# HGRN2 attention with a cosine router: embeddings' norm first, loads in order of use, a PSUM bank for the places, a clamp inside the scan, and the last three steps written out

## The chip, the cores and the metric

The kernel runs on one core of a Trainium2 chip. The metric is the device time of one execution in microseconds (us), measured for the kernel before and after the change; lower is better. The profile is one execution recorded by the hardware profiler. Its engines are TensorE (PE for matmuls, PEld for its weight loads), VectorE (DVE), ScalarE (ACT), GpSimd (POOL) and SyncE (SP, which issues most transfers). A name with a q behind it (SPq, ACTq, POOLq) is an engine's instruction queue.

## The reference

```python
def _attn_ref(q, k, v, f_logit):          # (4, 8, 768, 48): batch, heads, steps in time, head size
    f = 1.0 / (1.0 + np.exp(-f_logit))
    for t in range(S):
        state = f[:, :, t, :, None] * state + np.einsum('bhd,bhe->bhde', k[:, :, t], v[:, :, t])
        y[:, :, t] = np.einsum('bhd,bhde->bhe', q[:, :, t], state)

def _moe_ref(x, expert_emb, tau, w1, w2): # x: 3072 rows of 384, 8 experts, hidden size 1024
    xn = x / (np.linalg.norm(x, axis=-1, keepdims=True) + 1e-06)
    en = expert_emb / (np.linalg.norm(expert_emb, axis=-1, keepdims=True) + 1e-06)
    logits = xn @ en.T / tau
    expert_idx = np.argmax(logits, axis=1)
    gate_w = softmax(logits)[np.arange(N), expert_idx]
    for e in range(E):
        mask = expert_idx == e
        h = np.maximum(x[mask] @ w1[e], 0.0)
        out[mask] = gate_w[mask, None] * (h @ w2[e])
```

Gated linear attention gives 3072 rows of 384 numbers; each row goes to the one expert whose embedding is nearest by cosine, and comes back weighted by its gate. All data is fp32.

## The kernel before

The work is cut into 24 steps: six chunks of 128 positions, and in each chunk the four batches; step i is chunk i // 4 of batch i % 4, with all eight heads. Within a chunk the recurrence is turned into matrix products; a state of 48 by 48 per head is carried from chunk to chunk of a batch, that is, from step i to step i + 4.

Per step, by function: `load` brings f, k, q and v (192 KB each) by four transfers on SP. `decays` transposes f on TensorE (L676), takes its sigmoid on ACT into `f_T` (L684), and a scan on VectorE from the back forms the suffix products `suf` (L686). Their first column per head pair, the decay of the whole chunk, is clamped from below at `PC_MIN` into `pc_all` (L690), and its reciprocal (L694) starts the forward scan `at` (L700, `decays2`). `keys` transposes k, copies it out on ACT (`kraw`, L722) and multiplies it by `suf` on POOL into `kz` (L724). `queries` multiplies the transposed q by `at` into `qa` (L732). `carry` multiplies the incoming state by the chunk's decay on POOL (`old`, L709) and copies it on ACT into two halves of `st` (L714). `scores` multiplies `kz` by `qa` (L742) and masks on VectorE (`am`, L745). `outputs` multiplies `st` and v with `qa` and `am` into `f_y` (L788, L794), copied to `f_xT` on ACT (L799; `xT` below). `update` and `update2` transpose `kz` again (L757), copy it (`kt`, L759), multiply it by v into PSUM tile `add` (L770) and form the new state (`new`, L778).

Routing: `rows_out` turns `f_xT` back into rows together with the logits (L805, PSUM tile `misc`) and copies them out on ACT (`f_xg`, L811; squares, L813); `logits` sums the logits on VectorE (L817). After each group of steps (four, later two and one) `route` and `count` find the experts and the running counts on VectorE (L828 to L844; one copy on ACT), `place` counts the places of the group's rows by two matmuls (L851, L852, also in `misc`) and two VectorE operations (L854, L856), and `scatter` sends one step's rows to their place in `x_sorted` by an indirect transfer on POOL (L861). PSUM has eight banks: three for `tp`, and one each for `misc`, two `sc`, `add` and `f_y`.

The order is written out by hand: `as_written` keeps every engine to the program's order, and the loop at L983 calls the functions above for steps i + 2 down to i - 2, so a step passes through four rounds. In round i POOL gets the `kz` of step i + 1, one scatter and `old` of step i; the embeddings' norm and the tables of the router are worked out in round -1 (`tables`, `embeddings`). The norm (L914 to L924) uses a square on ACT and, on VectorE, four Newton steps for the root.

After the last step the expert stage follows: for each of eight experts its 448 places are read from `x_sorted` (L1048), transposed (L1057), multiplied by w1 (L1089) and w2 (L1103), and scattered to the output (L1118). Its first transposes wait for all rows. A flag (L1027 to L1039) starts a general path if an expert has too many rows or a decay was clamped; with these inputs it is not taken.

```python
                for i in range(-2, LAST + 1):
                    at(i + NLD, lambda j: load(j) if j >= NLD - 1 else None)
                    at(i + 2, decays)
                    at(i, update)
                    at(i + 1, keys)
                    at(i - 2, rows_out)
                    at(i + 1, queries)
                    at(i + 2, decays2)
                    at(i, carry)
                    at(i, scores)
                    at(i - 1, outputs)
                    at(i, update2)
```

Of the kernel before, what the change touches and what calls it, by code (L numbers as in the profile page):

```python
# [10 lines left out]
FP32 = mybir.dt.float32  # L11
# [534 lines left out]
def kernel(  # L546
# [53 lines left out]
    with ExitStack() as fast:  # L600
# [43 lines left out]
        with tc.tile_pool(name="f_fix", bufs=1) as fix, tc.tile_pool(name="f_work", bufs=2) as work, tc.tile_pool(  # L644
# [11 lines left out]
            cnt_ps = misc[:, HP * RW + B * E : HP * RW + B * E + E]  # L656
            bad_ps = misc[:, HP * RW + B * E + E : HP * RW + B * E + E + 1]
# [8 lines left out]
            def load(i):  # L666
                b, c = steps[i]
                for nm, src in (("f", f_logit), ("k", k), ("q", q), ("v", v)):
                    dst = lds[nm][i % len(lds[nm])][:, :, 0:DH]
                    nc.sync.dma_start(out=dst, in_=src[b, :, c * P : c * P + P].rearrange("h p d -> p h d"))  # L670
                live[i]["v"] = lds["v"][i % NV]
# [7 lines left out]
            def decays(i):  # L679
# [82 lines left out]
            def update2(i):  # L762
# [4 lines left out]
                add = ps_s.tile([P, HP, DH], FP32, name="add")  # L767
# [78 lines left out]
            def place(g):  # L846

                s0, n = groups[g]
                rank = misc[:, HP * RW : HP * RW + n * E].rearrange("p (e b) -> p e b", e=E)
                before = hots[g] if n == 1 else upto[g]  # L850
                nc.tensor.matmul(rank, lhsT=tri, rhs=hots[g][:, :, 1:], start=True, stop=False)  # L851
                nc.tensor.matmul(rank, lhsT=ones, rhs=before[:, :, 0:n], start=False, stop=True)  # L852
# [22 lines left out]
            def pads(j):  # L875
                for nm in "fkqv":
                    if j < len(lds[nm]):
                        nc.vector.memset(lds[nm][j][:, :, DH:64], 30.0 if nm == "f" else 0.0)

            def blanks(t):  # L880
                nc.gpsimd.memset(t, 0.0)

            def first():
                warm = work.tile([1, 1], FP32, name="f_warm", bufs=1)
                nc.vector.memset(warm, 0.0)
                nc.scalar.activation(warm, warm, AF.Sigmoid)
                for j in range(NLD - 1):
                    load(j)
                pads(0)
                blanks(f_sb[0])  # L890
                blanks(f_sb[1])
                pads(1)
                nc.vector.memset(revone, 0.0)
                nc.vector.memset(revone[:, 0 : HP * W].rearrange("p (n w) -> p n w", w=W)[:, :, 0], 1.0)
                nc.vector.memset(revone[:, HP * W : HP * W + 1], 1.0)
                blanks(fwd1[0])
                blanks(f_sb[2])
                blanks(fwd1[1])
                make_upper_triangular(nc, causal, val=1.0, diag=True)
                for j in range(2, NV):  # L900
                    pads(j)
                nc.vector.memset(emb[:, :, DH:64], 0.0)
                nc.scalar.dma_start(out=emb[:, :, 0:DH], in_=moe_expert_emb.rearrange("e (h d) -> e h d", h=H))
                nc.scalar.dma_start(out=tau, in_=moe_tau.to_broadcast([P, 1]))

            def embeddings():

                rtau = work.tile([P, 1], FP32, name="f_rtau", bufs=1)
                esq = work.tile([E, H, 64], FP32, name="f_esq", bufs=1)
# [266 lines left out]
```

## Time and profile before

| | us |
|---|---|
| median of 3 runs | 536.28 (536.28 to 536.43) |
| the profiled execution | 536.07 |
| its span, first to last instruction | 534.2 |
| TensorE matmuls busy | 476.6 (89%) |
| VectorE busy | 209.4 (39%) |
| ACT busy | 155.9 (29%) |
| POOL busy | 111.6 (21%) |
| mean granted TensorE clock | 0.963 |

The span is counted from the first instruction; the execution takes 1.87 us more. The busy shares are means over stages of different kind: TensorE's 89% holds in the expert stage as in the steady loop, while VectorE, ACT and POOL do most of their work in the first 200 us. What bounds a stage is read from its order of time: which wait ends last there. A row of the timeline gives the start in us from the span's start, the duration (of merged neighbours: from the first start to the last end), engine, line, operation, what it writes and reads, how many were merged, and, in brackets, the idle time of the engine before it with what ended that. A matmul's end is modelled; starts are firm. "issue" as the releaser means that the profile names none.

### The profile page before, as it was taken

The numbers are of one execution on the slowest core, as the hardware profiler recorded it, in microseconds if no ns is written. First come the engines' busy times: TensorE is split into PE (matmuls) and PEld (weight loads), VectorE is DVE, ScalarE is ACT, GpSimd is POOL, SyncE is SP. The second block draws the span as 40 slices with busy tenths as digits, with TensorE's granted clock in tenths as the row PEclk, the third lists the DMA queues.
The fourth block names the chain that finished last, engine by engine and source line by source line (L and its number), as shares of the span: only waits on it lengthen the run. The fifth ranks groups of instructions, "written<-read, shape, count | busy, mean of one in ns | idle before, by whom it ended". The sixth has DMA issues, their size and how long they took to land.

```text
span 534.2 us, 7556 instructions
## 1 busy us (share of the span) xinstructions
PE 476.6 (89%) x2968; PEld 314.4 (59%) x2968; DVE 209.4 (39%) x492; ACT 155.9 (29%) x330; POOL 111.6 (21%) x131
## 2 busy tenths in 40 slices
PE   2499899999898646999999999999999999999980
PEld 2398798989897544555555555555555555555540
DVE  7799789888886224331120220220220200201000
ACT  2156455555554223221221221221221201101210
POOL 3324254545453320000020110200200200200201
PEclk9999899999998875999999999999999999999995
DMA  9999999999710115053153143233323403100101
GB/s 145 163 164 219 195 274 232 187 316 191 132 41 19 61 63 161 1 171 118 21 196 118 54 161 118 96 121 118 110 108 118 148 17 119 41 1 0 44 3 52
DMA packets 117268, 61.64 MB, mean 115 GB/s; under 512 B 101568, under 2 KB 111225, under 8 KB 117224
## 3 DMA queue, kind: packets, MB, share of 16 engines
q1 hardware_dynamic: 113424, 51.42, 42.6%
q0 software_dynamic: 3584, 9.64, 5.3%
q8 instruction: 25, 0.41, 0.4%
q14 instruction: 19, 0.16, 0.1%
q10 hardware_dynamic: 216, 0.01, 0.0%
HBM read 49.79 MB, written 12.06 MB: 116 GB/s over the span
## 4 chain that ended last, share of the span: by engine, by line
issue 33%; PE 29%; POOL 3%; ACT 1%; DMA 1%; POOLq 0%; DVE 0%; SPq 0%; ACTq 0%; DVEq 0%
PE h_ps L1089 14%; PE y_ps L1103 10%; POOL out_dram L1118 3%; PE x_tp L1057 1%; PE misc L805 1%; DMA xs<-x_sorted 1%; PE sc L742 1%; PE f_y L788 1%; PE y_tp L1115 1%; PE f_y L794 1%; DMA x_sorted<-f_xg,f_pos_i 0%; ACT f_xT L799 0%; ACT f_yo L1117 0%; ACT f_xg L811 0%; PE misc L851 0%
## 5 line engine op out<-in xcount | busy, mean ns | idle before, releaser
L1089 PE MATMUL h_ps<-xTs,w 128*128 128x448 f32 x384 | 147.6, 545 | 0.0
L1103 PE MATMUL y_ps<-hTs,w 128*128 128x448 f32 x384 | 147.2, 540 | 0.0
L1089 PEld LDWEIGHTS h_ps<-xTs,w 128*128 128x128 f32 x384 | 73.8, 192 | 72.1 <-issue 71.7
L1103 PEld LDWEIGHTS y_ps<-hTs,w 128*128 128x128 f32 x384 | 71.7, 190 | 65.4 <-issue 65.4
L1118 POOL DMA_INDIRECT out_dram<-f_yo,gtok x32 | 30.2, 942 | 296.6 <-ACT f_yo L1117 291.7
L1093 DVE TENSOR_SCALAR hTs<-h_ps 128x448 f32<-128x448 f32 x32 | 20.0, 624 | 159.3 <-PE h_ps L1089 159.3
L724 POOL TENSOR_TENSOR kz<-kraw,suf 128x512 f32<-128x512 f32 x24 | 30.5, 1272 | 92.3 <-ACT kraw L722 40.5
L1095 ACT ACTIVATE hTs<-h_ps 128x448 f32<-128x448 f32 x32 | 17.4, 543 | 104.2 <-PE h_ps L1089 104.2
L1109 ACT COPY yTs<-y_ps 128x448 f32<-128x448 f32 x16 | 8.5, 532 | 117.5 <-PE y_ps L1103 117.5
L686 DVE TENSOR_TENSOR_SCAN suf<-f_T,revone 128x517 f32<-128x517 f32 x24 | 31.6, 1317 | 16.1 <-ACT f_T L684 16.0
L805 PE MATMUL misc<-unit,f_xT 128*128 128x104 f32 x192 | 26.9, 284 | 8.0 <-ACT f_xT L799 7.7
L700 DVE TENSOR_TENSOR_SCAN at<-f_T,fwd 128x516 f32<-128x516 f32 x24 | 31.2, 1300 | 0.0
L745 DVE TENSOR_TENSOR am<-sc,causal 128x512 f32<-128x512 f32 x48 | 30.6, 677 | 1.6 <-PE sc L742 1.6
L742 PE MATMUL sc<-qa,kz 64*128 64x128 f32 x384 | 30.9, 306 | 0.0
L805 PEld LDWEIGHTS misc<-unit,f_xT 128*128 128x128 f32 x192 | 23.7, 194 | 11.3 <-ACT f_xT L799 10.8
L861 POOL DMA_INDIRECT x_sorted<-f_xg,f_pos_i x24 | 25.1, 1046 | 22.2 <-issue 13.3
L714 ACT COPY st<-old 64x192 f32<-64x192 f32 x40 | 14.0, 350 | 50.7 <-POOL old L709 44.2
L742 PEld LDWEIGHTS sc<-qa,kz 64*128 64x128 f32 x384 | 26.1, 207 | 4.4 <-issue 3.2
L794 PE MATMUL f_y<-am,f_v 128*64 128x128 f32 x384 | 25.4, 275 | 0.0
L676 PE MATMUL tp<-f_ident,f_f 128*128 128x128 f32 x96 | 17.1, 304 | 8.0 <-DMA f_f<-in_f_logit_dram 4.1
L788 PE MATMUL f_y<-qa,st 128*64 128x128 f32 x320 | 23.2, 290 | 0.0
L794 PEld LDWEIGHTS f_y<-am,f_v 128*64 128x64 f32 x384 | 21.8, 138 | 0.5
(129 smaller groups left out, 462.0 us busy)
## 6 DMA issues: line engine op xcount, KB each, us to landing
w<-in_moe_w_dram SPq DMA_DIRECT2D x16, 1536.0 KB
xs<-x_sorted SPq DMA_DIRECT2D x8, 700.0 KB
f_f<-in_f_logit_dram SPq DMA_DIRECT2D x24, 192.0 KB
f_k<-in_k_dram SPq DMA_DIRECT2D x24, 192.0 KB
f_q<-in_q_dram SPq DMA_DIRECT2D x24, 192.0 KB
f_v<-in_v_dram SPq DMA_DIRECT2D x24, 192.0 KB
x_sorted<-blank SPq DMA_DIRECT2D x1, 1600.0 KB
out_dram<-f_yo,gtok POOLq DMA_INDIRECT x32, 5.5
```

The lines of the kernel that those rows point to most:

```text
L686: nc.vector.tensor_tensor_scan(suf[:, ::-1], ft[:, ::-1], revone[:, ::-1], 0.0, ALU.mult, ALU.add)
L700: nc.vector.tensor_tensor_scan(at, L["ft"][:, 0 : HP * W], L["d1"], 0.0, ALU.mult, ALU.add)
L724: nc.gpsimd.tensor_tensor(kz, kraw, z, ALU.mult)
L742: nc.tensor.matmul(sc[par][:, hp], lhsT=kz[r, hp], rhs=qa[r, hp], start=True, stop=True)
L745: nc.vector.tensor_tensor(am[:, par], sc[par], causal.unsqueeze(1).to_broadcast([P, HP, P]), ALU.mult)
L788: nc.tensor.matmul(y[r, hp], lhsT=L["st"][:, hp, par], rhs=L["qa"][:, hp], start=hp == 0, stop=False, skip_group_check=True,)
L794: nc.tensor.matmul(y[r, hp], lhsT=L["v"][:, 2 * hp + par], rhs=L["am"][:, par, hp], start=c == 0 and hp == 0, stop=True, skip_group_check= ...
L805: nc.tensor.matmul(rows_ps[:, hp], lhsT=L["xT"][:, hp], rhs=unit[:, hp], start=True, stop=True)
L861: nc.gpsimd.indirect_dma_start(out=x_views[s][:], out_offset=bass.IndirectOffsetOnAxis(ap=pos_i[:, s : s + 1], axis=0), in_=live[s]["row"] ...
L1089: nc.tensor.matmul(ps, lhsT=w1[:, c, f * P : f * P + P], rhs=xTs[e][:, c], start=c == 0, stop=c == DC - 1)
L1103: nc.tensor.matmul(ps, lhsT=w2[:, f, d * P : d * P + P], rhs=hTs[e][:, f], start=f == 0, stop=f == FC - 1)
L1118: nc.gpsimd.indirect_dma_start(out=out_views[e * NB + j][:], out_offset=bass.IndirectOffsetOnAxis(ap=gtok[:, e, j : j + 1], axis=0), in_=y ...
```

## The change

- Start (`first`): the transfer of the embeddings goes first on SP, f of step 1 is issued from ACT's queue, tau behind it. The embeddings' norm (square, root by ACT's table and one Newton step in `inv_norm`, scaling) is done ahead of the first step on ACT and VectorE. ACT first loads the table for roots, then that for sigmoids.
- Loads: `load` brings one tensor; each round asks for k, then f of the step after, then q and v. The pads of the load buffers, the router's tables and the other constants are written in rounds -1 to 3 by `prepare`, behind the round's other work, the pads from buffer 2 on by POOL in place of VectorE. The embeddings' transposes are in round 0, in `misc`.
- Clamp: the suffix scan multiplies and takes the maximum with `revone`, whose zeros are now `PC_MIN`. The VectorE instruction at L690 is gone; the reciprocal reads `suf`, and `pc_all` is a copy on ACT, behind the sigmoid of the step.
- PSUM: `add`, the places and the counts share a bank of their own, `small`; `misc` keeps the rows and the logits. The two matmuls of `place` change places.
- Order: `carry` is called for step i + 1 and ahead of the scatter. The loop ends at round 22, and what is left of the last three steps is written out, with scatters sent as their places are known.

```diff
-            cnt_ps = misc[:, HP * RW + B * E : HP * RW + B * E + E]
+            small = ps_s.tile([P, 512], FP32, name="small")
+            add_ps = small[:, 0 : HP * DH].rearrange("p (n d) -> p n d", d=DH)
+            rank_ps = small[:, HP * DH : HP * DH + B * E]
...
                 nc.vector.tensor_tensor_scan(
-                    suf[:, ::-1], ft[:, ::-1], revone[:, ::-1], 0.0, ALU.mult, ALU.add
-                )
-                pc = pc_all[:, i]
-                nc.vector.tensor_scalar(
-                    pc, suf[:, 0 : HP * W].rearrange("p (n w) -> p n w", w=W)[:, :, 1], PC_MIN, None, ALU.max
-                )
+                    suf[:, ::-1], ft[:, ::-1], revone[:, ::-1], 0.0, ALU.mult, ALU.max
+                )
+                pc = suf[:, 0 : HP * W].rearrange("p (n w) -> p n w", w=W)[:, :, 1]
                 d1 = fwd1[i % 2]
                 nc.vector.reciprocal(d1.rearrange("p (n w) -> p n w", w=W)[:, :, 0], pc)
+                nc.scalar.copy(pc_all[:, i], pc)
...
-                rank = misc[:, HP * RW : HP * RW + n * E].rearrange("p (e b) -> p e b", e=E)
+                rank = rank_ps[:, 0 : n * E].rearrange("p (e b) -> p e b", e=E)
...
             def first():
...
+                nc.vector.memset(en, 1.0)
+                nc.scalar.activation(en[0:1, 2:3], en[0:1, 2:3], AF.Sqrt)
+                nc.sync.dma_start(out=emb[:, :, 0:DH], in_=moe_expert_emb.rearrange("e (h d) -> e h d", h=H))
+                nc.vector.memset(emb[:, :, DH:64], 0.0)
+                load("f", 0)
+                load("f", 1, nc.scalar)
+                load("k", 0)
+                load("q", 0)
+                load("v", 0)
+                load("k", 1)
+                load("f", 2)
+                load("q", 1)
+                load("v", 1)
+                for j in range(2, NLD - 1):
+                    for nm, o in (("k", 0), ("f", 1), ("q", 0), ("v", 0)):
+                        load(nm, j + o)
+                nc.scalar.dma_start(out=tau, in_=moe_tau.to_broadcast([P, 1]))
...
+                nc.vector.memset(revone, PC_MIN)
...
+                nc.scalar.activation(esq, emb, AF.Square, accum_out=en[:, 0:1])
+                nc.vector.reciprocal(rtau, tau)
+                inv_norm(en[:, 1:2], en[:, 0:1], en[:, 2:3])
+                nc.scalar.activation(esq[0:1, 0, 0:1], esq[0:1, 0, 0:1], AF.Sigmoid)
+                nc.vector.tensor_scalar(emb, emb, en[:, 1:2], rtau[0:E], ALU.mult, ALU.mult)
...
+            def prepare(i):
+
+                if i == -1:
+                    pads(2, nc.gpsimd)
+                    pads(3, nc.gpsimd)
+                if i == 0:
+                    embeddings()
+                    pads(4, nc.gpsimd)
...
             with as_written(tc):
                 first()
-                for i in range(-2, LAST + 1):
-                    at(i + NLD, lambda j: load(j) if j >= NLD - 1 else None)
+                for i in range(-2, NST - 1):
+                    if i >= -1:
+                        for nm, o in (("k", 0), ("f", 1), ("q", 0), ("v", 0)):
+                            load(nm, i + NLD + o)
...
                     at(i - 2, logits)
-                    for s in ready[: 1 if i < NST - 4 else None]:
-                        scatter(s)
-                        ready.remove(s)
-                    at(i, carry)
+                    at(i + 1, carry)
+                    send(1 if i < NST - 4 else 2)
                     at(i, scores)
                     at(i - 1, outputs)
...
                     at(i, update2)
-                for g in pend:
-                    place(g)
-                    ready += range(groups[g][0], groups[g][0] + groups[g][1])
-                for s in ready:
-                    scatter(s)
+                    prepare(i)
+                scores(NST - 1)
+                rows_out(NST - 3)
+                settle()
+                outputs(NST - 2)
+                logits(NST - 3)
+                finish(NST - 3)
+                send(2)
+                outputs(NST - 1)
+                settle()
+                rows_out(NST - 2)
+                logits(NST - 2)
+                finish(NST - 2)
+                settle()
+                send(3)
+                rows_out(NST - 1)
+                logits(NST - 1)
+                finish(NST - 1)
+                settle()
+                send(B)
```

`settle` places the groups that are counted, `send(n)` scatters up to n steps whose places are known, and `finish(i)` routes and counts a group whose last step is i.

POOL in the steady loop before, two rounds in the middle of the loop (the DMA is the scatter of one step's rows):

```order
L724 TENSOR_TENSOR kz<-kraw,suf 128x512
L861 DMA x_sorted<-f_xg_82,f_pos_i 3584x400
L709 TENSOR_TENSOR old<-new,pc_all 128x192
L724 TENSOR_TENSOR kz<-kraw,suf 128x512
L861 DMA x_sorted<-f_xg_82,f_pos_i 3584x400
L709 TENSOR_TENSOR old<-new,pc_all 128x192
```

and in the changed kernel, the same rounds:

```order
L731 TENSOR_TENSOR kz<-kraw,suf 128x512
L716 TENSOR_TENSOR old<-new,pc_all 128x192
L868 DMA x_sorted<-f_xg_81,f_pos_i 3584x400
L731 TENSOR_TENSOR kz<-kraw,suf 128x512
L716 TENSOR_TENSOR old<-new,pc_all 128x192
L868 DMA x_sorted<-f_xg_81,f_pos_i 3584x400
```

`old` has moved from behind the scatter to ahead of it.

ACT over one steady round before, from one sigmoid to the next:

```order
L684 ACTIVATE f_T_146<-tp 128x4x128
L759 COPY f_kt<-tp 128x512
L722 COPY kraw<-tp 128x512
L811 COPY f_xg_82<-misc 128x384
L813 ACTIVATE f_sq,f_xg_82<-f_xg_82 128x384
L714 COPY st_143<-old 64x4x48 x2
```

and in the changed kernel:

```order
L693 ACTIVATE f_T_148<-tp 128x4x128
L701 COPY pc_all<-suf 128x4
L766 COPY f_kt<-tp 128x512
L729 COPY kraw<-tp 128x512
L818 COPY f_xg_81<-misc 128x384
L820 ACTIVATE f_sq,f_xg_81<-f_xg_81 128x384
L721 COPY st_142<-old 64x4x48 x2
```

The copy of `pc_all` from `suf` is new and stands ahead of `kt` and `kraw`.

ACT at the start before and, in the second fence, in the changed kernel:

```order
L886 ACT_TABLE_LOAD
L886 ACTIVATE f_warm<-f_warm 1x1
L903 DMA f_emb<-in_moe_expert_emb_dram 8x8x48
L904 DMA f_tau<-in_moe_tau_dram 128x1
L684 ACTIVATE f_T_145<-tp 128x4x128
```

```order
L895 ACT_TABLE_LOAD
L895 ACTIVATE f_en<-f_en 1x1
L676 DMA f_f_128<-in_f_logit_dram 128x8x48
L910 DMA f_tau<-in_moe_tau_dram 128x1
L922 ACTIVATE f_esq,f_en<-f_emb 8x512
L628 ACTIVATE f_en<-f_en 8x1
L925 ACT_TABLE_LOAD
L925 ACTIVATE f_esq<-f_esq 1x1
L693 ACTIVATE f_T_146<-tp 128x4x128
```

The square and root of the embeddings, and a second table load, now stand ahead of the first sigmoid of the data.

## Rows read from the trace of the kernel before

**Rows 1.** Windows, steady loop: PE PEld DVE ACT POOL busy, PEclk, DMA, GB/s.
```profile
51.30:163.20 111.90, 103.52 (x1395) 95.30 (x1394) 95.01 (x164) 60.61 (x150) 52.20 (x48) 0.98 0.91 196
```

**Rows 2.** Timeline of the start: us, duration, engine, line, op, tiles, count, [idle, releaser].
```profile
3.88 1.09 PE L676 MATMUL tp<-f_ident,f_f 128*128 128x128 f32 x4 [3.88 <-POOL causal masks.py:65]
...
5.70 1.24 DVE L686 TENSOR_TENSOR_SCAN suf<-f_T,revone 128x517 f32<-128x517 f32 x1 [0.33 <-ACT f_T L684]
...
9.10 1.09 PE L676 MATMUL tp<-f_ident,f_f 128*128 128x128 f32 x4 [4.13 <-DMA f_f<-in_f_logit_dram]
...
21.08 0.49 PEld L928 LDWEIGHTS tp<-f_ident,f_emb 8*128 8x128 f32 x4 [9.59 <-issue]
...
21.61 1.11 PE L676 MATMUL tp<-f_ident,f_f 128*128 128x128 f32 x4
...
37.50 0.66 PE L676 MATMUL tp<-f_ident,f_f 128*128 128x128 f32 x4
```

**Rows 3.** Timeline, ACT, first gates of the experts: a table load.
```profile
205.24 1.28 ACT L628 ACT_TABLE_LOAD   x1 [12.14 <-DMA xs<-x_sorted]
...
206.54 0.20 ACT L628 ACTIVATE g_rn<-g_sq 112x4 f32<-112x4 f32 x1
```

**Rows 4.** Timeline, one step of the steady loop.
```profile
102.45 1.01 DVE L690 TENSOR_SCALAR pc_all<-suf 128x4 f32<-128x4 f32 x1
...
103.58 1.01 POOL L861 DMA_INDIRECT x_sorted<-f_xg,f_pos_i  x1 [0.15 <-DVE pc_all L690]
...
104.16 1.37 DVE L700 TENSOR_TENSOR_SCAN at<-f_T,fwd 128x516 f32<-128x516 f32 x1
...
104.62 1.20 POOL L709 TENSOR_TENSOR old<-new,pc_all 128x192 f32<-128x192 f32 x1
...
105.85 0.72 ACT L714 COPY st<-old 64x192 f32<-64x192 f32 x2 [2.71 <-POOL old L709]
...
107.07 0.60 ACT L684 ACTIVATE f_T<-tp 128x512 f32<-128x512 f32 x1
...
108.78 1.18 POOL L724 TENSOR_TENSOR kz<-kraw,suf 128x512 f32<-128x512 f32 x1 [2.96 <-issue]
```

**Rows 5.** Timeline, end of the loop: scans beside POOL.
```profile
155.84 1.23 DVE L686 TENSOR_TENSOR_SCAN suf<-f_T,revone 128x517 f32<-128x517 f32 x1 [0.64 <-ACT f_T L684]
...
156.42 1.64 POOL L724 TENSOR_TENSOR kz<-kraw,suf 128x512 f32<-128x512 f32 x1 [2.46 <-issue]
...
158.79 1.22 DVE L700 TENSOR_TENSOR_SCAN at<-f_T,fwd 128x516 f32<-128x516 f32 x1
...
160.81 0.52 POOL L709 TENSOR_TENSOR old<-new,pc_all 128x192 f32<-128x192 f32 x1
```

**Rows 6.** Timeline, first places, and windows view behind them.
```profile
59.49 0.41 PE L851 MATMUL misc<-hot,f_tri 128*128 128x32 f32 x2 [2.13 <-ACT f_xg L811]
...
61.00:64.40 3.40, 3.40 (x36) 3.17 (x34) 2.86 (x5) 0.70 (x2) 1.71 (x2) 0.52 1.28 193
```

**Rows 7.** Timeline, VectorE: `suf` of steps 7 and 23.
```profile
51.26 1.85 DVE L686 TENSOR_TENSOR_SCAN suf<-f_T,revone 128x517 f32<-128x517 f32 x1
...
163.21 1.24 DVE L686 TENSOR_TENSOR_SCAN suf<-f_T,revone 128x517 f32<-128x517 f32 x1 [1.92 <-ACT f_T L684]
```

**Rows 8.** Timeline: TensorE in one steady step, then the tail.
```profile
100.90 1.04 PE L805 MATMUL misc<-unit,f_xT 128*128 128x104 f32 x8
...
105.19 0.62 PE L770 MATMUL add<-f_v,f_kt 128*64 128x48 f32 x16
...
178.15 0.71 ACT L714 COPY st<-old 64x192 f32<-64x192 f32 x2 [6.27 <-issue]
...
179.52 1.32 PE L805 MATMUL misc<-unit,f_xT 128*128 128x104 f32 x8 [4.14 <-ACT f_xT L799]
...
196.31 0.97 POOL L861 DMA_INDIRECT x_sorted<-f_xg,f_pos_i  x1 [1.00 <-issue]
...
204.67 2.71 PE L1057 MATMUL x_tp<-f_ident,xs 112*128 112x112 f32 x12 [7.17 <-DMA xs<-x_sorted]
```

More of the change, by code (lines that the diff above doesn't have):

```diff
@@ L664, with load @@
             state = {}
-            def load(i):
+            srcs = {"f": f_logit, "k": k, "q": q, "v": v}
+            def load(nm, i, queue=None):
+                if not 0 <= i < NST:
+                    return
                 b, c = steps[i]
[L668 to L671, printed above, removed]
+                t = lds[nm][i % len(lds[nm])]
+                (queue or nc.sync).dma_start(
+                    out=t[:, :, 0:DH], in_=srcs[nm][b, :, c * P : c * P + P].rearrange("h p d -> p h d")
+                )
+                if nm == "v":
+                    live[i]["v"] = t
             def turn(src):
@@ L883, in first @@
+            tok_i = work.tile([P, NST], I32, name="f_tok_i", bufs=1)
             def first():
[L884 to L893, printed above, removed]
+                rtau = work.tile([P, 1], FP32, name="f_rtau", bufs=1)
+                esq = work.tile([E, H, 64], FP32, name="f_esq", bufs=1)
+                en = work.tile([E, 3], FP32, name="f_en", bufs=1)
+                nc.vector.memset(en, 1.0)
[15 more added lines that the diff above has]
+                nc.scalar.dma_start(out=tau, in_=moe_tau.to_broadcast([P, 1]))
+                nc.gpsimd.memset(f_sb[0], 0.0)
+                nc.gpsimd.memset(f_sb[1], 0.0)
+                nc.gpsimd.memset(fwd1[0], 0.0)
+                nc.gpsimd.memset(fwd1[1], 0.0)
+                nc.gpsimd.memset(f_sb[2], 0.0)
+                make_upper_triangular(nc, causal, val=1.0, diag=True)
+                pads(0, nc.vector)
+                nc.vector.memset(revone, PC_MIN)
@@ L980, with settle, send, finish @@
             ready, pend = [], []
+            def settle():
+                for g in pend:
+                    place(g)
+                    ready.extend(range(groups[g][0], groups[g][0] + groups[g][1]))
+                pend.clear()
+            def send(n):
+                for s in ready[:n]:
+                    scatter(s)
+                del ready[:n]
+            def finish(i):
+                if i in done:
+                    route(done[i])
+                    count(done[i])
+                    pend.append(done[i])
             with as_written(tc):
                 first()
-                for i in range(-2, LAST + 1):
-                    at(i + NLD, lambda j: load(j) if j >= NLD - 1 else None)
-                    if i == 3:
+                for i in range(-2, NST - 1):
+                    if i >= -1:
+                        for nm, o in (("k", 0), ("f", 1), ("q", 0), ("v", 0)):
+                            load(nm, i + NLD + o)
+                    if i == 4:
                         fill()
-                    if i in (7, 12):
-                        weights(i // 12)
+                    if i in (8, 13):
+                        weights(i // 13)
                     at(i + 2, decays)
```

119 lines of the change are left out of this document (44 added, 75 removed).

## The prediction

> **What bounds the kernel now.** The profile was read from coarse to fine: stages, then the chain of waits, then the order of time around it. The expert stage, from its first transposes at 204.67 [rows 8] to 534.2, is left alone by the diff, so everything rests on when it starts. Three parts lead there.
>
> The start: the suffix scan `suf` of step 0 begins at 5.70, but the transposes of step 2, which open the full loop, come at 21.61. Ahead of them TensorE idles 9.59 us for the embeddings' transposes [rows 2]: their norm is worked out on VectorE behind the scans of two steps.
>
> The steady loop: from `suf` of step 7 to that of step 23 it takes 163.21 - 51.26 = 111.95 us for 16 steps, 7.00 each [rows 7]. TensorE is busy for 93% of the stretch [rows 1], but what repeats is a ring through POOL and ACT [rows 4]: `kz` ends, then the scatter, then `old`, which takes 1.20 us (0.52 where no scan runs beside it [rows 5]) and ends just behind the scan `at` (105.53); then the two `st` copies and `xT` (1.22 from `st` to `f_T`), then `f_T`, `kt`, `kraw` (1.71 from `f_T` to `kz`). VectorE cannot run ahead: the clamp `pc`, four elements, lasts 1.01 us and ends when `kz` does [rows 4]. Every fourth step adds the places: their matmuls find PSUM bank `misc` taken by the copy of the rows, 2.13 us of idle TensorE at 59.49 [rows 6].
>
> The tail: 41.46 us from `suf` 23 to the experts [rows 7, 8]. ACT idles 6.27 us before `st` at 178.15, since four scatters stand ahead of `old` on POOL.
>
> **The start, part by part.** The emb transfer goes first on SP, f of step 1 leaves by ACT's queue, and tau stands behind it there. The norm's first operation on VectorE waits for tau; then ACT does a square root, a second table load and a dummy sigmoid, and `f_T` 0 is queued behind all of them. Tau's landing shows nowhere in the trace. One load has landed and is read at 3.88, five at 9.10 [rows 2], 1.3 us per load; tau has two to three ahead of it, so I take 6.4, between 5.2 (one and a bit) and 9.1 (as if behind five). Then two small VectorE operations 0.25, root 0.20, table load until the next activation 1.30 [rows 3], dummy 0.20, `f_T` 0.60: `suf` 0 begins at 9.0 instead of 5.70, a loss of 3.3.
>
> Of the table, the rows show the next activation 1.30 us after the load began [rows 3]. The Trainium skill (ScalarE: Activation LUTs, What ACT_TABLE_LOAD costs) gives 2.66 us for each switch, a drain of 1.38 included; by it the sum would be 520.9. The trace agrees on the load, 1.28, and shows no such drain.
>
> From 9.0: `suf` 0 to 10.25, its `at` to 11.7, `suf` 1 (its sigmoid stands behind the copy of `pc` 0) to 13.0, `at` 1 from 13.7 to 14.9. `kz` 0 asks for its operands at 13.9, in the middle of that scan, and so ends about 1 us after it (next part), at 15.9; behind it POOL now writes the pad of f 2, so step 2's transposes start at 16.2 instead of 21.61. From there to the transposes of f 5 the trace took 15.9 us [rows 2]; I add 0.5 for the embeddings' transposes, now in between, and 0.7 for `kz` held up twice: 33.3 instead of 37.50. Gain 4.2.
>
> **The steady loop.** `old` and `st` are now those of the next step and stand before the scatter, so the scatter (1.01 us and its hops) leaves the ring. But `pc` is now a copy on ACT that waits for `suf` and stands before `kt` and `kraw`. So `kz` asks for its operands about 1.37 us after `suf` ends (0.15 for the copy, 1.22 of today's 1.71). Without the clamp VectorE starts `at` 0.70 after `suf` (today 0.70 after `pc`: 103.46 to 104.16 [rows 4]) and gets there first. One pair shows what follows: `suf` ran undisturbed from 155.84 to 157.07, `kz`, begun at 156.42, took 1.64 us and ended 0.99 after it [rows 5]. The new ring, from the end of `suf`: 0.70, `at` 1.22, `kz` 0.99, `old` 0.52 [rows 5], hop 0.03, `st` to `f_T` 1.22, `f_T` 0.60, hop 0.04, `suf` 1.24: **6.56 us**. TensorE stays below: 4.29 from rows to the state's matmuls [rows 8], these 0.62, three transposes at some 0.4, about 6.1. Of four steps one carries the copy of the counts (0.11), one the two place operations ahead of `qa` (0.34): 26.7 per four, 106.8 for 16, against 111.95. Here the own bank counts: the places no longer wait for the copy, and the stretch after that idle, granted 0.52, about the 1.2 GHz level [rows 6], should not come. Gain 5.15.
>
> Of the pair, `kz` needed 0.99 of its usual 1.18 us after the scan. The Trainium skill (SBUF — State Buffer, Who interferes with whom) says that whichever engine starts first keeps the shared pair for its whole instruction and the other fully blocks; with a full 1.18 behind the scan a step would be 6.75 and the sum 522.5. The row shows a part of the time already spent, so 0.99 stands.
>
> Between f 5 and `suf` 7 the ring sets in a step earlier than before, as `old` does: `suf` 5 at 34.6 (f 5 plus transposes 0.66, `f_T` 0.60, hop), `suf` 7 at 47.7 against 51.26, so 3.55 of the 4.2 is left. `suf` 23 begins at 47.7 + 106.8 = 154.5: 8.7 gained in all.
>
> **The tail.** `xT` of step 20 ends 4.8 us after `suf` 23 ends, as in the ring; then TensorE does rows, q, scores and outputs (4.29 [rows 8]), the places 0.45 and the last scores 1.1. With `suf` itself 1.24, rows of step 21 start 11.8 after `suf` 23 begins, against 179.52 - 163.21 = 16.3: the scatters stand behind both `old`. Gain 4.5. From those rows to the experts the trace took 25.15 [rows 8]; I take 1.1 off for the last scores, now ahead, 1.8 for the last outputs, which now run beside row copies, 0.5 for places that no longer wait behind a copy. The last 8.36, from the last scatter to the experts, stay. Gain 3.4, with ends 0 (nothing overlaps, or TensorE's clock falls again in new gaps) and 6.
>
> **At no cost.** SP's new load order: loads are issued five steps ahead, some 30 us, which hides it; without that cover 1.3 us per load. Pads and tables on POOL stand behind `kz` in steps 0 to 3, where POOL has one `kz` per step; uncovered, about 3 us once. The scan with max in place of add: no row shows one. Below, nothing in the rows suggests a gain; above, rival (d) has the price. I take no change, since `suf` and `at` last the same 1.2 us with different operands.
>
> **Sum.** 8.7 + 4.5 + 3.4 = 16.6 off the profiled execution's 536.07 (534.2 of span, 1.87 around it): **519.5 us**. That execution lies 0.21 us below the median 536.28.
>
> **Rivals.** (a) `at` is late, because `qa` waits over 0.67 us for its transposes: then `kz` goes first, `at` next, and `old` is held behind `at` as today. The ring grows by 0.65, 16 steps by 10.4: 529.9. For it: that is how the pair stands now [rows 4]. Against: in the new ring the transposes of q end before `suf` does. (b) `kz` is not held by `at`: the ring falls to TensorE's 6.1, 7.4 less: 512. For it: `kz` and `at` never meet in today's loop, so rows 5 are one case with another scan. (c) Tau lands at 9.1, or the pads hold up the first steps: the start loses 2.7 to 5: 522 to 524.5. (d) Slower: the scan with max is the longer operation. `suf` lies on the ring once a step, so 0.1 us costs 2.4 over 24 steps; from 0.69 more (1.24 to 1.93) the gain is gone, at double length the time is 519.5 + 24 x 1.24 = 549. Against: the equal scans above. (e) The change doesn't do what it says: POOL is a whole scatter late, so `st` still waits for one and the loop keeps 7.00; the gain is 3.55 + 7.9: 524.6.
>
> **How the numbers follow.** Forecast 0.58 (514 to 524 by the ends of tau and tail), (a) 0.13, (b) 0.11, (c) 0.07, (d) 0.04, (e) 0.07. The range 511 to 528 leaves out (a) and (d). Over 0.2%, some 1.1 us, is about what a measurement of this kernel can tell from no change: faster 0.94, same 0.02, slower 0.04, from (d) and its near misses.
>
> **What would show it.** Right: `suf` 0 near 9.0, step 2's transposes near 16, `suf` rows 6.5 to 6.6 apart, `kz` lasting 1.5 or more and ending 1 us behind `at`, `old` at 0.52, no half clock before the tail, the experts' first transposes near 188. Wrong: `old` near 1.2 (a); `kz` at 1.18 and steps near 6.1 (b); `suf` 0 after 11 (c); `suf` over 1.24 (d); a scatter between `kz` and `old` (e).

## The result, and the profile after

The changed kernel takes 517.74 us (median of 4 runs, 515.62 to 519.3) against 536.28: a ratio of 0.9658, 95% interval 0.9619 to 0.9697, 18.5 us less. The profiled execution took 518.0, its span 516.1. The 18.1 us between the two spans, by the marks of the prediction:

| stretch | before | after | gain | forecast |
|---|---|---|---|---|
| start to `suf` 7 | 51.26 | 46.50 | 4.76 | 3.55 |
| `suf` 7 to `suf` 23 | 111.95 | 107.76 | 4.19 | 5.15 |
| `suf` 23 to rows of step 21 | 16.31 | 12.08 | 4.23 | 4.5 |
| these rows to the experts' transposes | 25.15 | 20.87 | 4.28 | 3.4 |
| experts to the end | 329.53 | 328.89 | 0.64 | 0 |

The start, in the timeline of the changed kernel (columns as in [rows 2]); the last two rows are `suf` 7 and `suf` 23:

```profile
4.61 0.16 DVE L923 RECIPROCAL f_rtau<-f_tau 128x1 f32<-128x1 f32 x1 [1.77 <-DMA f_tau<-in_moe_tau_dram]
...
5.19 0.14 DVE L627 TENSOR_SCALAR f_en<-f_en 8x1 f32<-8x1 f32 x1 [0.41 <-ACT f_esq L922]
5.36 0.20 ACT L628 ACTIVATE f_en<-f_en 8x1 f32<-8x1 f32 x1 [0.21 <-DVE f_en L627]
5.58 1.28 ACT L925 ACT_TABLE_LOAD   x1
...
5.72 1.94 PE L685 MATMUL tp<-f_ident,f_f 128*128 128x128 f32 x8 [5.72 <-DMA f_f<-in_f_logit_dram]
...
6.88 0.20 ACT L925 ACTIVATE f_esq<-f_esq 1x1 f32<-1x1 f32 x1
6.98 0.57 ACT L693 ACTIVATE f_T<-tp 128x512 f32<-128x512 f32 x1
...
7.59 1.23 DVE L695 TENSOR_TENSOR_SCAN suf<-f_T,revone 128x517 f32<-128x517 f32 x1 [0.54 <-ACT f_T L693]
...
12.30 2.17 POOL L731 TENSOR_TENSOR kz<-kraw,suf 128x512 f32<-128x512 f32 x1 [8.16 <-ACT kraw L729]
...
14.66 1.12 PE L685 MATMUL tp<-f_ident,f_f 128*128 128x128 f32 x4 [5.30 <-POOL f_f L885]
...
46.50 1.23 DVE L695 TENSOR_TENSOR_SCAN suf<-f_T,revone 128x517 f32<-128x517 f32 x1 [1.80 <-ACT f_T L693]
...
154.26 1.23 DVE L695 TENSOR_TENSOR_SCAN suf<-f_T,revone 128x517 f32<-128x517 f32 x1 [2.12 <-ACT f_T L693]
```

Tau is read at 4.61 and holds nothing up: the operation ahead of the root, at 5.19, waits for the squares of the embeddings on ACT. The first `suf` is at 7.59, and step 2 opens at 14.66 in place of 21.61, released by the pad that POOL writes behind `kz` 0.

One steady step of the changed kernel, to be held against [rows 4]:

```profile
94.58 1.24 DVE L695 TENSOR_TENSOR_SCAN suf<-f_T,revone 128x517 f32<-128x517 f32 x1 [1.50 <-ACT f_T L693]
95.84 0.20 ACT L701 COPY pc_all<-suf 128x4 f32<-128x4 f32 x1 [1.30 <-DVE suf L695]
...
96.52 1.22 DVE L707 TENSOR_TENSOR_SCAN at<-f_T,fwd 128x516 f32<-128x516 f32 x1
...
97.16 1.57 POOL L731 TENSOR_TENSOR kz<-kraw,suf 128x512 f32<-128x512 f32 x1 [3.31 <-issue]
...
98.69 0.50 POOL L716 TENSOR_TENSOR old<-new,pc_all 128x192 f32<-128x192 f32 x1
...
99.23 0.72 ACT L721 COPY st<-old 64x192 f32<-64x192 f32 x2 [1.18 <-POOL old L716]
...
99.35 1.01 POOL L868 DMA_INDIRECT x_sorted<-f_xg,f_pos_i  x1 [0.16 <-issue]
...
100.45 0.60 ACT L693 ACTIVATE f_T<-tp 128x512 f32<-128x512 f32 x1
...
101.09 1.23 DVE L695 TENSOR_TENSOR_SCAN suf<-f_T,revone 128x517 f32<-128x517 f32 x1 [1.50 <-ACT f_T L693]
```

This is the forecast ring, term by term: `at` starts 0.70 after `suf` ends (95.82), `kz` ends 0.99 after `at` (98.73 against 97.74), `old` takes 0.50, `st` to `f_T` 1.22, and the next `suf` comes 6.51 after the one before. Four steps take 26.58 (88.07 to 114.65), against a forecast of 26.7 and 27.3 before. TensorE is granted full clock throughout the loop.

One step breaks the pattern, 60.06 to 67.98, 7.92 us:

```profile
54.34 1.21 SPq L984 DMA_DIRECT2D x_sorted<-blank  x1
...
63.24 1.17 POOL L868 DMA_INDIRECT x_sorted<-f_xg,f_pos_i  x1 [5.07 <-DVE at L707]
...
64.44 1.19 POOL L731 TENSOR_TENSOR kz<-kraw,suf 128x512 f32<-128x512 f32 x1
```

The first scatter stands on POOL ahead of `kz`, and POOL idles 5.07 us before it. The profile names `at`. The other candidate is the fill of the unused rows of `x_sorted` (the first row), which takes 8.0 us to land. The experiments below tell these apart.

The tail, from the rows of step 21 to the last scatter and the experts, and the clock (windows view, columns as in [rows 1]):

```profile
166.34 1.14 PE L812 MATMUL misc<-unit,f_xT 128*128 128x104 f32 x8
...
178.83 0.97 POOL L868 DMA_INDIRECT x_sorted<-f_xg,f_pos_i  x1 [1.56 <-issue]
...
187.21 2.70 PE L1095 MATMUL x_tp<-f_ident,xs 112*128 112x112 f32 x12 [7.19 <-DMA xs<-x_sorted]
```

```profile
46.50:154.26 107.76, 104.25 (x1403) 94.61 (x1402) 78.83 (x148) 63.94 (x167) 49.87 (x48) 1.00 1.02 211
...
178.00:182.00 4.00, 1.12 (x4) 0.93 (x4) 0.96 (x7) 0.00 (x0) 0.97 (x1) 0.50 0.22 83
```

### The profile page after: what moved, and what is told of

Read it like the earlier page. It is cut to its first block, busy times and chain, and to the rows that moved or that the text cites. A ratio compares the mean times of both kernels' runs of the same rounds, so it can differ in the third digit from the quotient of the medians.

```text
span 516.1 us, 7516 instructions
## 1 busy us (share of the span) xinstructions
PE 471.3 (91%) x2968; PEld 309.0 (60%) x2968; DVE 184.2 (36%) x439; ACT 160.5 (31%) x357; POOL 113.3 (22%) x149
## 4 chain that ended last, share of the span: by engine, by line
issue 58%; POOL 5%; PE 3%; DMA 1%; ACT 1%; POOLq 0%; DVE 0%; SPq 0%; DVEq 0%
POOL out_dram L1156 4%; DMA xs<-x_sorted 1%; PE misc L812 1%; PE f_y L795 1%; PE f_y L801 1%; DMA x_sorted<-f_xg,f_pos_i 1%; PE sc L749 0%; POOL x_sorted L868 0%; POOL old L716 0%; POOLq L1156 0%; ACT f_xT L806 0%; ACT f_xg L818 0%; PE small L859 0%; ACT st L721 0%; PE small L858 0%
## 5 line engine op out<-in xcount | busy, mean ns | idle before, releaser
L731 POOL TENSOR_TENSOR kz<-kraw,suf 128x512 f32<-128x512 f32 x24 | 39.4, 1643 | 79.1 <-ACT kraw L729 44.3
L695 DVE TENSOR_TENSOR_SCAN suf<-f_T,revone 128x517 f32<-128x517 f32 x24 | 29.6, 1232 | 33.1 <-ACT f_T L693 33.1
L749 PE MATMUL sc<-qa,kz 64*128 64x128 f32 x384 | 28.8, 291 | 0.0
L749 PEld LDWEIGHTS sc<-qa,kz 64*128 64x128 f32 x384 | 24.1, 193 | 4.2 <-issue 4.2
L795 PE MATMUL f_y<-qa,st 128*64 128x128 f32 x320 | 21.9, 279 | 0.7 <-ACT f_xT L806 0.7
L1155 ACT ACTIVATE f_yo<-y_tp,f_gate 112x384 f32<-112x384 f32 x32 | 16.8, 577 | 16.7 <-PE y_tp L1153 15.1
```

What stands on the lines that cost most here:

```text
L695: nc.vector.tensor_tensor_scan(suf[:, ::-1], ft[:, ::-1], revone[:, ::-1], 0.0, ALU.mult, ALU.max)
L731: nc.gpsimd.tensor_tensor(kz, kraw, z, ALU.mult)
L749: nc.tensor.matmul(sc[par][:, hp], lhsT=kz[r, hp], rhs=qa[r, hp], start=True, stop=True)
L795: nc.tensor.matmul(y[r, hp], lhsT=L["st"][:, hp, par], rhs=L["qa"][:, hp], start=hp == 0, stop=False, skip_group_check=True,)
```

## Experiments

All are edits of the changed kernel but the last, which is one of the kernel before. Times are medians; the ratio is to the kernel before on the same chip.

### What the order on POOL and ACT is worth

The scatter put back ahead of `carry`, which stays that of the next step:

```diff
-                    at(i + 1, carry)
                     send(1 if i < NST - 4 else 2)
+                    at(i + 1, carry)
```

> The changed kernel with the scatter ahead of carry again, carry still that of the next step. Theory (the ring runs from kz over old to st, xT and the next f_T): the scatter, 1.01 us and about 0.3 of gaps, comes back into it for 16 to 17 steps; suf rows 7.6 to 7.8 apart in place of 6.50, some 20 us more, 535 to 539. Rival (the ring is set by TensorE or by VectorE with its scans, and POOL has room): suf rows stay 6.5 apart and the time within 2 us of 517.7.

546.92 us, ratio 1.0185 (1.0152 to 1.0218). Its steps, in the timeline:

```profile
110.26 1.58 POOL L731 TENSOR_TENSOR kz<-kraw,suf 128x512 f32<-128x512 f32 x1 [4.46 <-issue]
...
112.00 1.01 POOL L868 DMA_INDIRECT x_sorted<-f_xg,f_pos_i  x1 [0.16 <-issue]
...
113.03 0.52 POOL L716 TENSOR_TENSOR old<-new,pc_all 128x192 f32<-128x192 f32 x1
```

`suf` rows are 7.75 apart in steps without places, as the ring says. With this line alone undone, the changed kernel is slower than the kernel before. The time exceeds the expectation by 8: in one step of 14.50 the first scatter, waiting for the fill of `x_sorted` (below), now holds `old` too, and the stretch from `suf` 23 to the experts takes 3.7 more.

The copy of `pc_all` moved behind `kraw`:

```diff
-                nc.scalar.copy(pc_all[:, i], pc)
...
                     at(i + 1, keys)
+                    at(i + 2, decays1)
```

(`decays1` is that copy.)

> The changed kernel with the copy of pc_all on ACT behind kraw in place of ahead of kt. Theory: kt and kraw no longer wait for suf, so kz begins just before suf ends, ahead of at; kz ends about 1 us behind suf, at begins some 0.8 later, and old at 0.5 us fits between the two; st comes 1.2 to 1.8 us earlier and the step falls to what TensorE or VectorE need, 6.1 to 6.2: 6 us gained over 17 steps, 510 to 513. Rival A: at begins before old, so old takes 1.2 beside it as in the kernel before, the step stays at 6.5 and the time at 517 to 518. Rival B: the copies of pc_all now hold old: the step grows.

515.34 us, ratio 0.9599 (0.9563 to 0.9635). Ordinary steps fall to 6.21:

```profile
101.63 1.18 POOL L733 TENSOR_TENSOR kz<-kraw,suf 128x512 f32<-128x512 f32 x1 [2.43 <-issue]
...
102.72 1.22 DVE L709 TENSOR_TENSOR_SCAN at<-f_T,fwd 128x516 f32<-128x516 f32 x1
...
102.78 1.47 POOL L718 TENSOR_TENSOR old<-new,pc_all 128x192 f32<-128x192 f32 x1
```

`kz` runs ahead of `at`, at its undisturbed 1.18. `old` does take 1.47 beside `at`, as rival A had it, but the step still falls: `kz` no longer waits for `at`, and no gap is left on TensorE in this step. Of the expected 6 us only 2.4 arrive, because the step at the fill grows to 16.33 us. Here the profile names the cause itself:

```profile
64.02 1.16 POOL L870 DMA_INDIRECT x_sorted<-f_xg,f_pos_i  x1 [15.39 <-DMA x_sorted<-blank]
```

The clamp as a VectorE instruction again:

```diff
-                    suf[:, ::-1], ft[:, ::-1], revone[:, ::-1], 0.0, ALU.mult, ALU.max
+                    suf[:, ::-1], ft[:, ::-1], revone[:, ::-1], 0.0, ALU.mult, ALU.add
...
+                nc.vector.tensor_scalar(
+                    pc, suf[:, 0 : HP * W].rearrange("p (n w) -> p n w", w=W)[:, :, 1], PC_MIN, None, ALU.max
+                )
...
-                nc.scalar.copy(pc_all[:, i], pc)
```

> The changed kernel with the clamp as its own VectorE instruction again (suffix scan with add, no copy on ACT). Theory (the copy on ACT that waits for suf is what puts kz behind at in the changed ring, and the scan with max costs nothing of its own): kz runs beside suf's end again, the clamp ends with kz at about 1 us behind suf, at begins 0.7 later, old fits in between at 0.5; the step falls to 6.1 to 6.3, 4 to 6 us gained: 512 to 514. So the clamp's part of the change would have cost time, not saved it. Rival (the clamp inside the scan is one of the sources of the gain): the step grows to 7 or more, as VectorE is held for 1 us again: 525 or more. suf itself lasts 1.23 either way.

516.55 us, ratio 0.9628 (0.9591 to 0.9665). Steps of 6.0 to 6.2, 6.88 with the places, and 11.76 at the fill. `suf` lasts 1.23 with either operation. The time is that of the changed kernel within the spread of the runs, so the clamp inside the scan brings nothing that shows in this order of ACT. The same edit with the scatters later, so that none waits for the fill:

```diff
-                    send(1 if i < NST - 4 else 2)
+                    send((0 if i < 9 else 2 if i < 11 else 1) if i < NST - 4 else 2)
```

> The changed kernel with the clamp as its own VectorE instruction again, and the scatters from round 9. Without the late scatters its steps were 6.0 to 6.2 and 6.88 with the places, but one of 11.76 held the fill of x_sorted. Theory: that one falls to 6.2, the loop runs as in the run with pc_all behind kraw (6.2 and 6.6), so that the clamp inside the scan is worth 1 us or less once its copy does not hold kt and kraw: 506 to 509. Rival (VectorE, held 1 us a step by the clamp, becomes the bound): 511 to 514.

510.79 us, ratio 0.9538 (0.9522 to 0.9554), between the two and nearer the rival: against the run with the copy behind `kraw` and the same scatters (506.53) the separate clamp costs 4.3 us. 3.0 of them are there by `suf` 7 (43.37 against 40.33). The rival's cause, VectorE as the bound, does not show: in the steady loop four steps take 25.26 in either run, and from 85 to 120 us TensorE is busy without a break in this one. In the tail this execution is 1.8 longer, with a stall that is shown under the fill of `x_sorted` and has no known cause. The clamp inside the scan thus pays at the start, once its copy is out of the way of `kraw`; that it pays in the steady loop isn't shown.

### The places' own bank

```diff
-            rank_ps = small[:, HP * DH : HP * DH + B * E]
+            rank_ps = misc[:, HP * RW : HP * RW + B * E]
```

(and the counts likewise)

> The changed kernel with the places and counts back in the bank misc, beside the rows. Theory: in the six rounds that place a group, the two matmuls wait again until ACT has copied the rows out (some 2.3 us behind the rows, since kt, kraw and the copy of pc_all stand ahead of that copy on ACT); the transposes of q, qa and the scan at stand behind them, so four steps of the loop grow from 6.8 by up to 2, and TensorE idles: some 8 us in the loop and 1 or more in the tail, 525 to 530. Rival (the wait is hidden, because the ring runs through ACT and POOL): 518 to 519.

535.74 us (530.5 to 538.86 in ten runs), ratio 0.9968 (0.9935 to 1.0001): the whole gain is gone. The wait is the expected one (waits view: engine, line, for what, total, times, longest), but behind it the granted clock fell (windows view):

```profile
PE misc L858 <- ACT f_xg L818: 10.7, 5, 2.5
```

```profile
113.00:116.70 3.70, 1.17 (x11) 0.99 (x10) 1.41 (x2) 2.29 (x8) 1.06 (x1) 0.98 1.13 227
116.70:120.10 3.40, 3.40 (x28) 2.85 (x28) 2.84 (x6) 0.70 (x2) 1.59 (x3) 0.52 0.99 370
```

In the loop the wait is 2.53 to 2.54 long in each of four steps; in the kernel before it was 2.13 once and 1.27 in the three steps after. One step with places took 8.76, two more 10.32 and 10.33: 1.9 for the idle time, and 1.6 more where the clock fell to the 1.2 GHz level, as it did once in the loop of the kernel before [rows 6]. The step of 8.76 had the same wait, at 87.30, and was granted the full clock. Undone by itself, the bank is worth 18 us; the prediction gave it 0.5 in the tail and no number of its own in the loop.

### The fill of x_sorted

```diff
-                    if i == 4:
+                    if i == 3:
                         fill()
```

> One line of the changed kernel: the transfer that fills the unused rows of x_sorted is asked for in round 3 in place of round 4. In the changed kernel it is issued at 54.34 us and takes a median 8.0, and the first scatter runs at 63.24, ahead of kz (64.44) on POOL; that step is 7.92 long where its neighbours take 6.50. Theory: the scatter waits for the fill, and kz behind it; with the fill four loads (some 4.9 us) earlier the scatter runs at about 58.4, the step falls to 6.5, and 1.4 us are gained: 516.3 against 517.7. Rival, as the releaser in the profile reads: the scatter waits for the end of the scan at on VectorE; then the scatter stays at 63.2 and the time at 517.7.

518.36 us, ratio 0.9651 (0.9617 to 0.9686): no gain in the time. But the step that holds the first scatter is as expected:

```profile
49.98 1.03 SPq L984 DMA_DIRECT2D x_sorted<-blank  x1
...
58.90 1.16 POOL L868 DMA_INDIRECT x_sorted<-f_xg,f_pos_i  x1 [0.93 <-DVE new L785]
```

It falls to 6.50, so the fill held the scatter. In the three runs where the profile names the fill as what the scatter waits for, the scatter comes 8.8 to 9.4 us behind the fill's issue; in the changed kernel it is 8.9. `suf` 23 begins at 152.67, 1.59 earlier than in the changed kernel. The gain is lost in the tail of that execution, where ACT starts 2.2 and VectorE 2.6 us after the matmuls that they wait for, beside four scatters:

```profile
163.65 1.16 PE L749 MATMUL sc<-qa,kz 64*128 64x128 f32 x16
...
165.89 0.59 ACT L806 COPY f_xT<-f_y 128x512 f32<-128x512 f32 x1 [3.77 <-PE sc L749]
...
167.41 1.29 DVE L752 TENSOR_TENSOR am<-sc,causal 128x512 f32<-128x512 f32 x2 [4.27 <-remote]
```

In the changed kernel, with the same four scatters there, these come 0.05 us after their matmuls. The same stall (1.2 to 3.2 us) stands in five more profiled executions: the first run with the copy behind `kraw`, both with the clamp apart, and, below, those with the weights and with the norm moved. What causes it isn't settled.

The pads of buffer 2 ahead of the first `kz`:

```diff
                 make_upper_triangular(nc, causal, val=1.0, diag=True)
+                pads(2, nc.gpsimd)
```

> The changed kernel with the pads of load buffer 2 written on POOL ahead of the first kz, where POOL idles from 4.1 to 12.3 us, in place of behind it. Theory: the transposes of step 2, at 14.66 in the changed kernel, wait for that pad alone; they come at 10 to 11.5 and suf of step 2 at 13.5 to 14 in place of 16.51, 2.5 to 3 gained there. But the first scatter still waits for the fill of x_sorted (issued at about 54.3 behind 40 loads, on a queue that runs without a break), so the gain is given back in the step that holds kz behind that scatter (7.92 grows to some 10): 517 to 518.5, the same as the changed kernel. Rival (the queue has slack, or the scatter does not wait for the fill): 515.

518.15 us, ratio 0.9649 (0.9618 to 0.9679). `suf` 2 comes at 13.60, 2.9 earlier, `suf` 7 at 45.05, 1.45 earlier. The two steps around the first scatter (63.92) take 10.03 and 7.90, and `suf` 11 comes at 76.54, later than the 74.48 of the changed kernel. What is gained ahead of the fill is given back at the fill, and in this execution (521.08, the highest of 4) more than that: TensorE idles 2.6 us for the `kz` behind the scatter, and the granted clock falls (0.86 and 0.74 over the two steps).

The copy behind `kraw`, and no scatter before round 9:

```diff
+                    at(i + 2, decays1)
...
+                    send((0 if i < 9 else 2 if i < 11 else 1) if i < NST - 4 else 2)
```

> The run with the copy of pc_all behind kraw, which had steps of 6.21 but one of 16.3 us, where the first scatter stood on POOL ahead of kz and waited 15.39 us for the fill of x_sorted: here the scatters begin three rounds later (none before round 9, two each in rounds 9 and 10). Theory: that step falls to 6.2, or to 9 if the loads behind the fill are late, 7 to 10 us gained over 515.3: 505 to 508. Rival (the loop has run into the queue of loads, and the fill only showed it): some stall stays where the loads of steps 10 and 11 land, 510 to 513.

506.53 us, ratio 0.9422 (0.9378 to 0.9467): the step of 16.33 is 6.20. This version beats both kernels. What is left in its loop are two steps of 7.47 and 9.51, where f waits behind the experts' weights. These transfers were moved in one more run, with the pads of buffer 2 early:

```diff
-                    if i in (8, 13):
-                        weights(i // 13)
+                    if i in (11, 17):
+                        weights(i // 17)
```

> The run with pc_all behind kraw and the scatters from round 9 (506.5 us), with the two transfers of expert weights asked for in rounds 11 and 17 in place of 8 and 13, and the pads of buffer 2 written ahead of the first kz. In the run before, two steps of 7.47 and 9.51 us (neighbours 6.2) wait 1.22 and 2.82 us on TensorE for f, whose transfer stands behind weights. Theory: both steps fall to 6.2 to 6.6 and some 4 us are gained, and 1 to 1.5 at the start, where the transposes of step 2 come at 10.5 in place of 11.86: 501 to 503. Rival (the weights then come late for the experts, or the start is bound by the loads): 503 to 506.

505.56 us, ratio 0.9432 (0.9416 to 0.9448): the loop from `suf` 7 to 23 takes 100.28 in place of 104.13, the expected 4, and the time is the same. The start did not gain: step 2 comes at 11.78 against 11.86, held in both runs by its own transfer ("2.38 <-DMA f_f") and not by the pad, and `suf` 7 comes 2.55 later (42.88 against 40.33), where the profile shows the 1.2 GHz level from 12.8 to 23.0 and the run before it had it for a third as long. In the tail the stall of ACT and VectorE came again. So the expectation failed, in the start and in the tail.

### The start and the tail

The embeddings' norm moved behind the work of round -1 (from `first` to `prepare`, with the first dummy activation a sigmoid):

```diff
-                inv_norm(en[:, 1:2], en[:, 0:1], en[:, 2:3])
...
                 if i == -1:
+                    inv_norm(en[:, 1:2], en[:, 0:1], en[:, 2:3])
```

> The changed kernel with the embeddings' norm behind the work of round -1 in place of ahead of the first step; its two table loads stand there too. Theory: suf of step 0 begins at about 7.4 in place of 7.59, since the transposes of f wait for their transfer until 5.72 anyway; the sigmoid of step 2 then waits behind root and table on ACT, suf of step 2 at 17 to 18 in place of 16.51, suf of step 7 at 47 to 48 in place of 46.50. The wait for the fill takes this up again in the step of 7.92, and the time is 517 to 519. Rival (the norm ahead is what brought the start's 4.76 us): suf of step 7 at 50 or later.

522.7 us (2 runs), ratio 0.9757 (0.9738 to 0.9777). `suf` 0 begins at 7.93 and `suf` 7 at 46.51, against 7.59 and 46.50: where the norm stands is worth nothing up to there. `suf` 23 is at 154.72, 0.46 late. Of the 4.5 us between the two profiled spans, 3.5 arise between `suf` 23 and the experts, where this execution shows both the 1.2 GHz level (granted 0.53 from 162.5 to 165.9) and the stall of ACT and VectorE. The order of the tail is the same in both kernels. But both runs of this one lie above all four of the changed kernel (515.62 to 519.3), so that the place of the norm has no part in the longer tail isn't shown.

The last three steps in the loop's order again:

```diff
-                for i in range(-2, NST - 1):
+                for i in range(-2, LAST + 1):
...
-                scores(NST - 1)
-                rows_out(NST - 3)
...
```

> The changed kernel with the last three steps in the loop's order again (two more rounds), carry still ahead of the scatters. Theory, by the prediction's terms: the 4.5 us up to the rows of step 21 stay, since they come from the place of carry; from those rows to the experts 3.4 us (4.3 as the changed kernel shows) are lost: 521 to 522. Rival (the gain behind rows 21 came from the places' own bank and the clock): within 1 us of 517.7.

517.68 us, ratio 0.9639 (0.9599 to 0.9679): the rival. In its profiled execution (520.36, the highest of 4) the experts begin 2.2 us later than in the changed kernel: 0.4 are there by `suf` 23, 1.25 arise from there to the rows of step 21, with the 1.2 GHz level from 162.7 to 166.1, and 0.6 behind those rows. The runs of either kernel spread over some 4 us, so no worth of the written-out tail can be told from the times.

### Two pieces alone in the kernel before

```diff
+            rank_ps = small[:, HP * DH : HP * DH + B * E]
...
-                    for s in ready[: 1 if i < NST - 4 else None]:
-                        scatter(s)
-                        ready.remove(s)
-                    at(i, carry)
+                    at(i + 1, carry)
+                    for s in ready[: 1 if i < NST - 4 else None]:
+                        scatter(s)
+                        ready.remove(s)
```

> The kernel before with two pieces of the change alone: the bank small for the state's product, the places and the counts, and carry of the next step ahead of the scatter. Start, order of loads, clamp and the last three steps as before. Theory (these two carry the gain; the clamp's part costs about what it saves, the written-out tail is worth under 2 us): steps of 6.0 to 6.2 and 6.9 with the places, 16 steps in 101 to 103 in place of 111.95, 7 to 8 less in the tail: 516 to 521, the changed kernel's own time, though the start is 4 us later. Rival (the parts add up as the prediction had it, and a clamp on VectorE holds the ring): 524 or more.

515.67 us (513.4 to 518.38), ratio 0.9634 (0.959 to 0.9677). The start is that of the kernel before (`suf` 7 at 50.85), but the 16 steps take 100.64, with TensorE busy for 99.83 of them, and the experts begin at 184.76, before the changed kernel's 187.21. One of its steps:

```profile
95.63 1.17 POOL L727 TENSOR_TENSOR kz<-kraw,suf 128x512 f32<-128x512 f32 x1 [3.38 <-issue]
...
95.82 1.01 DVE L693 TENSOR_SCALAR pc_all<-suf 128x4 f32<-128x4 f32 x1
...
96.77 0.50 POOL L712 TENSOR_TENSOR old<-new,pc_all 128x192 f32<-128x192 f32 x1
...
97.30 0.71 ACT L717 COPY st<-old 64x192 f32<-64x192 f32 x2 [0.51 <-POOL old L712]
...
97.53 1.22 DVE L703 TENSOR_TENSOR_SCAN at<-f_T,fwd 128x516 f32<-128x516 f32 x1
```

`old` fits between the clamp and `at`, which the scatter used to fill. These two pieces bring the whole gain; start, clamp, loads and written-out tail together add nothing to it that the runs can tell. By the traces that is a balance: the changed kernel is 4.35 ahead at `suf` 7 and 7.12 slower over the 16 steps. The two pieces were not put into the kernel before one at a time.

## Why the prediction was right, and where it was not

**The start.** The step that failed is tau at 6.4: it is read at 4.61. What `suf` 0 waits for is the transfer of f 0, which now stands behind the embeddings; its transposes start at 5.72. The norm's chain on ACT ends at almost the same time: with the norm moved away, `f_T` 0 starts 1.19 behind the transposes, here 1.26. So `suf` 0 lost 1.9 and not 3.3, and the gain at `suf` 7 was 4.76, not 3.55. Step 2 waiting for the pad behind `kz` 0 held (14.66 against a forecast of 16.2, most of the difference being `suf` 0). The table load cost what [rows 3] showed: 1.28, and the next activation 1.30 after its start. The 2.66 of the Trainium skill (ScalarE: Activation LUTs, What ACT_TABLE_LOAD costs) does not fit: the root before it ends at 5.56 and the load begins at 5.58, so no drain shows.

**The loop.** The ring of 6.56 measured 6.50. The forecast gain was 1.0 too high (4.19 against 5.15) for a reason that the prediction left out: the fill of `x_sorted`, moved a round later, holds the first scatter and with it `kz`, 1.42 us in one step; the other steps came out 0.46 better than forecast. "SP's new load order" at no cost was the failed step: issuing the loads early did hide it for them, but not for the transfer that stands behind 44 of them. Rival (e), a scatter still in the ring, did not come true, and the run with the scatter first shows what it would have cost. Rivals (a) and (b) did not come either, but (b)'s ring of 6.1 is what the run with the copy behind `kraw` gets (6.21): the copy on ACT, not TensorE, set the changed kernel's step. Rival (d), a longer scan with max, is excluded: 1.23.

**The pair of POOL and VectorE.** `kz` ended 0.97 to 0.99 after `at` whether it had begun with the scan (12.30) or 0.58 before its end (97.16). So the 0.99 of [rows 5] held, but it is no matter of how much time was already spent: some 0.2 of the 1.18 goes by during the wait, however long that is. `old` shows the same in the run with the copy behind `kraw`: 0.50 alone, it ended 0.31 after the `at` beside which it began. The Trainium skill (SBUF — State Buffer, Who interferes with whom) has the later instruction fully blocked while the first holds the shared pair. The trace agrees but for this 0.2.

**The tail.** 4.5 for `carry` ahead of the scatters measured 4.23, but the order is not the only cause: from `suf` 23 to the rows of step 21 the changed kernel takes 12.08, 14.17 with the scatter first, and 16.02 with the places back in `misc` (granted 0.50 from 175 to 179 us), close to the 16.31 before. The 3.4 behind it measured 4.28, but not for the reason given: with the tail in the loop's order all but 0.6 of it stays. Most of it comes with the places' bank and the order on POOL: the kernel before with these two alone takes 21.51 from the rows of step 21 (163.25) to the experts, against 25.15. Both count: the changed kernel takes 20.87 there, 22.49 with the scatter first and 23.11 with the places in `misc`.

**As a whole**, the time came out within 1.8 us of the forecast, and some of that is luck: the five stretches missed by +1.21, -0.96, -0.27, +0.88 and +0.64 us of gain, which partly cancel, and the pieces do not add up as the prediction had them. Taken out one by one, the order on POOL is worth 29 us and the bank 18, and together they are worth 20 in the kernel before.

## What to carry to other kernels

Write down the ring that repeats, engine by engine, and ask of each instruction in it whether anything later waits behind it in program order: here one scatter ahead of `old` and one copy ahead of `kraw` set the step. Look for a transfer behind a long queue first when a step is freed and the time does not move: in the eleven profiled kernels that ask for the fill in round 4 it was issued at 54.3 to 55.3 us, however early the steps ahead of it ran, and a scatter that waited for it took back what they had gained. Judge small edits by rows of the trace: in four executions with the same order of the tail the stretch from `suf` 23 to the experts took 32.95 to 36.45.

## What the runs showed of the hardware

In the run with the places in `misc` TensorE idled 2.53 to 2.54 us four times in the loop. After three of these the clock fell to the 1.2 GHz level (0.50 to 0.54 granted), which cost 1.6 us in a step; after the fourth, and after an idle time of 2.82 in the run with no scatter before round 9, it did not. In the changed kernel's loop, where no wait of TensorE for another engine is over 0.9 us, the clock was granted in full. POOL's issue of a scatter, 1.01 us alone, took 1.75 when it began beside `at` (in the run with the copy behind `kraw`). ACT and VectorE started 1.2 to 3.2 us late beside four scatters in the tail of six profiled executions, and 0.05 us behind their matmuls beside the same scatters in the changed kernel; the cause stays open.
